# Scores as native float32 products in two 64-row halves, in place of split float32r products

## The chip, the cores and the metric

The kernel runs on one core of a Trainium2 chip. The metric is the device time of one execution in microseconds (us); the time given is the median of the timed runs. PE is TensorE (its products), PEld its weight loads, DVE is VectorE, ACT ScalarE, POOL GpSimd, SP the sync engine, from whose queue the kernel issues its DMAs.

## The reference

Attention with a threshold over 4 batches of 8 heads (576 tokens, 64 columns), then a gated product with four weights, then a mixture of eight experts over all 2304 tokens.

```
scores = q @ k.T / sqrt(64)                          # per head, 576 x 576
thresh = max(scores, axis=-1) - tau
scores = where(scores >= thresh, scores, -1e9)
attn   = exp(scores - max(scores))
out    = attn / (sum(attn) + 1e-9) @ v               # 576 x 64 per head
x = out of all heads side by side                    # 2304 x 512
x = ((x @ w1) * (x @ w2)) @ w3 @ w_out
out = sum over 8 experts e: P[:, e] * (relu(x @ W1[e]) @ W2[e])
      # P from x @ w_gate, normalised over rows and columns 8 times
```

Everything is float32 at the inputs and the output (w1, w2, w3 and w_out are float64 and are turned into float32 on the chip).

## The kernel before

Two heads are one pair; there are 16 pairs. The 576 query rows of each head are cut into four tiles of 128 rows, and what is left of both heads (64 rows each) makes a ninth tile of 128 rows. So a pair is nine tiles, t = 0 to 8, and the attention part runs 144 steps, one per tile, after which the mixture stages follow. All instructions stand in an order written out by hand: each engine works through its own list in order, and a letter string, `ORDER`, says in which order the parts of a step are issued. The parts of one step belong to different tiles: in step s the mask of tile s (`mask`), the scores, the row maximum, the threshold and the exponential of tile s + 2 (`scores`, `rowmax`, `thresh`, `expo`), the transposes of tile s - 1 (`transp`, evacuated by `evac`), the transposes of the last 64 columns of three tiles (`tails`, every third step), the product with the values (`pv`, in steps t = 0, 2, 3, 5 and 7) and the spreading of the sums (`spread`, t = 2 and 8). The sum over the values (`vsum`) stands behind step t = 1.

On TensorE a step thus runs: transposes t (L205), scores s (L160), now and then rb (L281), tt (L216) and pv (L251), the filler products w (L487), and vs (L228). On VectorE it runs: the mask (L180), the reciprocal (L199), a piece of a weight's conversion to float32 (lines 516 to 524, one in most steps by `CONVERT`), the row maximum (L165), some of the parts of `prep`, and the product x (L300). The scores of two tiles have a PSUM buffer each, of two banks: the left 288 keys in one bank, the right 288 in the other. The scores of tile s + 2 wait until the mask of tile s has read its buffer.

A score in float32 accuracy is made of float32r products, which take fewer passes than float32 ones. Each head's q and k arrive with their 64 columns twice, on partitions 0 to 63 and 64 to 127. ScalarE rounds k to float32r (kh, L137) and GpSimd subtracts (kl, L140; VectorE does the very first). ScalarE writes q/8 rounded to float32r on all 128 partitions of qs (L129), and VectorE turns the lower 64 into the remainder (L133, two halves of 288 columns a head). One product of qs with kh and one with kl over 128 rows then give a block of 288 keys: four products a tile, and eight for the ninth tile, whose two heads accumulate into one result; for that, qs has 64 columns of zeros between the heads, and head 1's q is rotated by 64 rows in the input's layout. The parts of `prep` for pair n + 1 are spread over the steps of pair n by `PREP`: GpSimd's in t = 3 and 6, VectorE's (L133) in t = 4, 5, 7 and 8, ScalarE's in t = 0, 1, 4 and 5. `load` (L96, DMAs at L106) fetches q for pair n + 2 at t = 2 and k at t = 4, two DMAs each of 288 KB. Before the first step pair 0 is loaded in eight smaller DMAs, one head's k and q after the other, and pair 1 behind them.

Beside the attention, `W34` converts the float64 weights and multiplies w3 by w_out in small portions, spread over the steps.

Of the kernel before, what the change touches and what calls it, by code (L numbers as in the profile page):

```python
# [9 lines left out]
F32 = mybir.dt.float32  # L10
F32R = mybir.dt.float32r
AF = mybir.ActivationFunctionType
ALU = mybir.AluOpType
# [6 lines left out]
B, H, S, D = 4, 8, 576, 64  # L20
DM, DFF, E = 512, 1024, 8
NTOK = B * S
NP = B * H // 2
# [1 line left out]
SB = 768  # L25
HT = SB // 2
NSB = NTOK // SB
QW = 2 * S + 64

SPLITS_AT = ((0, 0), (1, 1), (2, 2), (3, 3), (8, 4), (9, 5), (10, 6))  # L30

# [1 line left out]

CONVERT = (1, 0, 1, 1, 1, 2, 1, 1, 1, 1, 1, 1, 1, 1, 2, 2, 1, 1)
PRODUCTS = (0, 4, 0, 0, 4, 0, 1, 0, 5, 0, 3, 0, 1, 4, 0, 2, 1, 4)
ORDER = "TfmzeiSVsqIovgrcxRltXyw"
PREP = {0: (4,), 1: (0,), 3: (6,), 4: (2, 1), 5: (3, 5), 6: (7,), 7: (8,), 8: (9,)}
PD = 2
SHARE = 2.0
AHEAD = {-2: 1, -1: 2, 0: 1, 1: 1, 2: 3, 3: 1, 4: 1, 5: 1, 6: 1, 7: 1}  # L40
# [11 lines left out]
def tile_of(n, t):  # L52

    return TILES[min(n, 1)][t]
# [9 lines left out]
def f32(ap):  # L64
    return ap.bitcast(F32)
# [6 lines left out]
def attention(k):  # L72

    tc, nc = k.tc, k.nc
# [3 lines left out]
    epool = early.enter_context(tc.tile_pool(name="atte", bufs=1))  # L78
# [14 lines left out]

    raws, sets = {}, {}

    def load(n, i):  # L96
        if n >= NP:
            return
        t = epool.tile([128, 2, S], F32, tag=f"r{i}", name=f"r{i}_{n}", bufs=2)
        raws[n, i] = t  # L100
        if n:
            fetch(n, i, slice(0, 2))

    def fetch(n, i, h):
        for half in range(2):
            nc.sync.dma_start(raws[n, i][64 * half:64 * half + 64, h], k.qk[n, :, 2 * i + h.start:2 * i + h.stop])  # L106

    def load_v(n):
        if n >= NP:
# [2 lines left out]
        nc.sync.dma_start(rv, k.vv[n])  # L112
        raws["v", n] = rv

    def prep(n, part):
        if n >= NP:
            return
        rq, rk = raws[n, 0], raws[n, 1]
        if n not in sets:
            qs = epool.tile([128, QW], F32R, tag="qs", name=f"qs{n}", bufs=2)  # L120
            kh = epool.tile([128, 2, S], F32R, tag="kh", name=f"kh{n}", bufs=2)
            kl = epool.tile([128, 2, S], F32R, tag="kl", name=f"kl{n}", bufs=2)
            sets[n] = (qs, kh, kl)
            nc.gpsimd.memset(f32(qs[:, S:S + 64]), 0.0)
        qs, kh, kl = sets[n]
        qcol = (slice(0, S), slice(S + 64, QW))
        if part in (0, 1):
            h = part
            nc.scalar.activation(qs[:, qcol[h]], rq[:, h], AF.Copy, scale=0.125)  # L129
        elif part in (2, 3, 8, 9):  # L130
            h, o = part % 2, 0 if part < 4 else 288
            dst = qs[64:128, qcol[h].start + o:qcol[h].start + o + 288]
            nc.vector.scalar_tensor_tensor(  # L133
                out=dst, in0=rq[64:128, h, o:o + 288], scalar=0.125, in1=f32(dst), op0=ALU.mult, op1=ALU.subtract)
        elif part in (4, 5):
            h = part - 4
            nc.scalar.activation(kh[:, h], rk[:, h], AF.Copy)  # L137
        elif part in (6, 7):
            h = part - 6
            (nc.gpsimd if n or h else nc.vector).tensor_tensor(out=kl[:, h], in0=rk[:, h], in1=f32(kh[:, h]), op=ALU.subtract)  # L140

    spool, ppool, tpool, outs = {}, {}, {}, {}

    def scores(s):
        if s >= NT:
            return
        n, t = divmod(s, 9)
        qs, kh, kl = sets[n]
        ps = psums.tile([128, 2, 512], F32, tag="s", name=f"s{s}", bufs=2)
        spool[s] = ps  # L150
        h, i = tile_of(n, t)
        if h is None:
            todo = [(512, 0), (576, 1)]
        else:
            todo = [((QW - 512 if h else 0) + 128 * i, h)]
        for c in range(2):
            cols = slice(288 * c, 288 * c + 288)
            ops = [(q0, h, kk) for q0, h in todo for kk in (kh, kl)]
            for i, (q0, h, kk) in enumerate(ops):
                nc.tensor.matmul(ps[:, c, 0:288], lhsT=qs[:, q0:q0 + 128], rhs=kk[:, h, cols],  # L160
                                 start=i == 0, stop=i == len(ops) - 1)

    def rowmax(s):
        ps = spool[s]
# [129 lines left out]
    def x_out(s):  # L294
        if (nj := due(s, "y")) is None:
# [4 lines left out]
        nc.vector.tensor_tensor(out=k.x[:, c0, S * b + q:S * b + q + m], in0=outs.pop((n, j))[:, 0:m],  # L300
                                in1=outs.pop(("r", n, j))[:, 0:m], op=ALU.mult)

    load(0, 1)
    load(0, 0)
    for h in range(2):
        fetch(0, 1, slice(h, h + 1))
        fetch(0, 0, slice(h, h + 1))
    nc.sync.dma_start(k.ntau, k.tau.to_broadcast([128, 1]))
    nc.scalar.activation(thr[:, 0:1], k.ident[:, 0:1], AF.Exp)
    fill = W34(k, epool, wpool, psum)  # L310
    load(1, 0)
    load(1, 1)
    for part in (4, 6, 0, 2):
        prep(0, part)
    nc.scalar.mul(k.ntau, k.ntau, -1.0)
    load_v(0)
    scores(0)
# [1 line left out]
    for s in range(2):  # L319
        rowmax(s)  # L320
        thresh(s)
        expo(s)
    for part in (1, 3, 5, 7):
        prep(0, part)

    def parts(s, which):
        n, t = divmod(s, 9)
        for part in PREP.get(t, ())[which]:
            prep(n + 1, part)

    def tiles(f, d):

# [2 lines left out]
    def groups(f, d):  # L335
# [6 lines left out]
        "q": groups(tails, 3), "l": groups(tail_out, 3), "v": pv,  # L342
        "V": spread, "I": repeat, "o": spread_out, "y": x_out, "f": lambda s: fill.out(),
        "c": lambda s: fill.convert(s, 2 if s < RAMP else CONVERT[s % 18]), "z": lambda s: fill.convert(s, 0),
        "r": lambda s: parts(s, slice(0, 1)), "R": lambda s: parts(s, slice(1, 9)), "w": lambda s: fill.mms(s)}
    ahead = iter(())
    for s in range(NT + 10):
        n, t = divmod(s, 9)
        if s == NT - 20:
            k.raw0 = wpool.tile([128, 4, 256], F32, name="raw1_0")  # L350
            nc.sync.dma_start(k.raw0.rearrange("p a b -> p (a b)"), k.wab["a"][0])
        if s >= NT - 2 and k.moe is None and fill.gen is None:
            early.close()
            k.moe = Moe(k)
            ahead = k.moe.run()
        if s == NT:
            banks.close()
            k.moe.banks()
        if s == NT + 1:
            assert fill.done()  # L360
            parts34.close()
            k.moe.grow()
        for what in ORDER:
            if what in steps:
                steps[what](s)
        if s < 2:
            prep(0, (9, 8)[s])
        if n < NP and t in (2, 4):
            load(n + 2, t // 2 - 1)
        if (s - SUMS_AT) % 9 == 0 and 0 <= s - SUMS_AT < NT:  # L370
            vsum((s - SUMS_AT) // 9)
        if n < NP and t == VALUES_AT:
            load_v(n + 1)
        if k.moe:
            for _ in range(AHEAD.get(s - NT, 0)):
                next(ahead)
# [7 lines left out]
class W34:  # L384
# [28 lines left out]
    def load(self, j):  # L413
        if j >= len(self.chunks):
            return
        raw = self.pool.tile([128, 512, 2], I32, tag="wraw", name=f"wraw{j}", bufs=2)
        self.k.nc.sync.dma_start(raw.rearrange("p a b -> p (a b)"), self.source(j).bitcast(I32))
        self.raw[j] = raw
# [544 lines left out]
def _layouts(np, inputs):  # L963

    c = np.ascontiguousarray
    pairs = lambda a: a.reshape(NP, 2, S, D)
    q = pairs(inputs["q"])
    q = np.stack([q[:, 0], np.roll(q[:, 1], 64, axis=1)], axis=1)
    qk = c(np.concatenate([a.transpose(0, 3, 1, 2) for a in (q, pairs(inputs["k"]))], axis=2))
    v = pairs(inputs["v"])  # L970
    vv = c(np.concatenate([v[:, :, :512].reshape(NP, 2, 4, 128, D), np.concatenate([v[:, :, 512:], np.zeros_like(v[:, :, 512:])], axis=2)[:, :, None]],
                          axis=2).transpose(0, 3, 1, 2, 4))
# [32 lines left out]
```

## Time and profile before

| | us |
|---|---|
| median of 3 runs (2286.64 to 2288.07) | 2287.48 |
| the profiled execution | 2283.88 |
| its span, first to last instruction | 2281.8 |
| mask of the first tile starts | 12.27 |
| mask of the last tile starts | 448.18 |

| engine | busy us | share of the span |
|---|---|---|
| PE | 2171.4 | 95% |
| PEld | 1945.2 | 85% |
| DVE | 1272.9 | 56% |
| ACT | 971.9 | 43% |
| POOL | 1074.0 | 47% |

The page of a profile gives one execution. Busy time of PE runs from the start of a product to its modelled end, and products overlap, so a busy PE isn't PE at its peak. L160 is line 160 of the kernel. In the views by line, "idle before" is the time in which the engine stood still ahead of these instructions, and the arrow names what ended it. Timelines merge equal neighbours (x16) and give the start of the first and the time until the end of the last.

### The profile page before, as it was taken

To read this page: it belongs to the slowest core of one execution; us is meant where nothing else is said; L and a number is where in the kernel's file an instruction comes from. 1 tells how busy PE (TensorE), PEld (TensorE's weight loads), DVE (VectorE), ACT (ScalarE), POOL (GpSimd) and SP (SyncE) were. 2 spreads that over 40 slices of the span, in tenths; PEclk is the share of its full clock that TensorE was granted. 3 is DMA by queue.
4 is the path that set the end of the run, shared out by engine and by line. 5 is a ranking of instruction groups with operands and counts; after the bars stand their busy time and mean duration, and the time that the engine had idled before them with its cause. 6 is when DMAs were issued, how large, how long until landed. Compare 5 with 4: busy or idle time off the path is not lost.

```text
span 2281.8 us, 32262 instructions
## 1 busy us (share of the span) xinstructions
PE 2171.4 (95%) x12624; PEld 1945.2 (85%) x12624; DVE 1272.9 (56%) x2175; ACT 971.9 (43%) x1805; POOL 1074.0 (47%) x1029
## 2 busy tenths in 40 slices
PE   6788888899999999999999999999999999999999
PEld 5677777788989888999999899999999899999998
DVE  7898988756464565444444644444445544444444
ACT  6787788743222333333333433333334333333332
POOL 4665666575010444444445544444446544444442
PEclk9999999999999999999999999999999999999999
DMA  5344344165435121211211211211211211211211
GB/s 145 100 118 133 111 137 128 48 254 189 189 148 189 49 73 56 75 66 65 74 65 65 102 66 64 74 66 64 74 68 63 102 67 64 74 69 61 74 69 43
DMA packets 57432, 213.39 MB, mean 94 GB/s; under 512 B 7104, under 2 KB 7104, under 8 KB 57280
## 3 DMA queue, kind: packets, MB, share of 16 engines
q1 hardware_dynamic: 57280, 211.33, 27.3%
q8 instruction: 99, 1.62, 0.3%
q14 instruction: 53, 0.43, 0.1%
HBM read 185.61 MB, written 25.69 MB: 93 GB/s over the span
## 4 chain that ended last, share of the span: by engine, by line
PE 69%; DVE 1%; issue 0%; ACT 0%; POOL 0%; DVEq 0%; ACTq 0%
PE ye L749 36%; PE py L679 19%; PE px L679 14%; DVE xl L668 0%; PE py L828 0%; DVE c L723 0%; PE px L828 0%; DVE c L734 0%; DVE prob L866 0%; ACT xh L667 0%; DVE acc L803 0%; POOL w1l L623 0%; DVE hl L745 0%; POOL w1l L620 0%; DVE small L863 0%
## 5 line engine op out<-in xcount | busy, mean ns | idle before, releaser
L749 PE MATMUL ye<-w2h,hl 128*128 128x512 f32 x1152 | 451.2, 392 | 0.0
L749 PE MATMUL ye<-w2h,hh 128*128 128x512 f32 x1152 | 451.1, 392 | 0.0
L749 PE MATMUL ye<-w2l,hh 128*128 128x512 f32 x1152 | 450.8, 391 | 0.0
L744 ACT ACTIVATE hh<-c 128x384 fp32r<-128x384 f32 x288 | 151.5, 526 | 611.0 <-DVE c L723 611.0
L625 POOL TENSOR_TENSOR w1l<-wt,w1h 128x1024 fp32r<-128x1024 f32 x104 | 252.6, 2429 | 285.4 <-ACT w1h L622 284.9
L679 PE MATMUL py<-xh,w1h 128*128 128x384 f32 x960 | 322.8, 336 | 7.5 <-DVE c L723 3.6
L679 PE MATMUL py<-xl,w1h 128*128 128x384 f32 x960 | 322.8, 336 | 3.5 <-DVE xl L668 3.5
L679 PE MATMUL py<-xh,w1l 128*128 128x384 f32 x960 | 322.0, 335 | 0.0
L620 POOL TENSOR_TENSOR w1l<-raw,w1h 128x256 fp32r<-128x256 f32 x104 | 79.2, 762 | 479.3 <-ACT w1h L614 479.3
L679 PE MATMUL px<-xh,w1h 128*128 128x384 f32 x720 | 242.6, 337 | 5.5 <-ACT p L703 2.8
L679 PE MATMUL px<-xl,w1h 128*128 128x384 f32 x720 | 242.1, 336 | 2.7 <-DVE xl L668 2.7
L749 PEld LDWEIGHTS ye<-w2l,hh 128*128 128x128 f32 x1152 | 216.3, 188 | 32.6
L749 PEld LDWEIGHTS ye<-w2h,hl 128*128 128x128 f32 x1152 | 216.2, 188 | 32.6
L679 PE MATMUL px<-xh,w1l 128*128 128x384 f32 x720 | 241.7, 336 | 0.0
L749 PEld LDWEIGHTS ye<-w2h,hh 128*128 128x128 f32 x1152 | 216.3, 188 | 24.6 <-ACT x L775 0.2
L679 PEld LDWEIGHTS py<-xh,w1h 128*128 128x128 f32 x960 | 180.2, 188 | 31.2 <-DVE c L723 6.5
L679 PEld LDWEIGHTS py<-xl,w1h 128*128 128x128 f32 x960 | 180.1, 188 | 22.3 <-DVE xl L668 5.3
L706 DVE TENSOR_TENSOR u<-py,p 128x384 f32<-128x384 f32 x120 | 66.8, 556 | 216.9 <-PE py L679 214.8
L160 PE MATMUL s<-kh,qs 128*128 128x288 f32 x320 | 106.5, 349 | 77.6 <-DVE p L180 70.5
L679 PEld LDWEIGHTS py<-xh,w1l 128*128 128x128 f32 x960 | 180.1, 188 | 0.0
L613 POOL TENSOR_TENSOR wt<-raw 128x512 f32<-128x512 f32 x104 | 139.4, 1340 | 76.9 <-DMA raw<-in_e 61.1
L745 DVE SCALAR_TENSOR_TENSOR hl<-c,hh 128x384 fp32r<-128x384 f32 x288 | 166.1, 577 | 9.3
(142 smaller groups left out, 4166.9 us busy)
## 6 DMA issues: line engine op xcount, KB each, us to landing
raw<-in_e SPq DMA_DIRECT2D x192, 512.0 KB, 4.0
r<-in_qk SPq DMA_DIRECT2D x60, 288.0 KB, 5.8
wraw<-in_w SPq DMA_DIRECT2D x32, 512.0 KB, 3.6
w1h<-w_kept SPq DMA_DIRECT2D x16, 896.0 KB, 5.0
w1l<-w_kept SPq DMA_DIRECT2D x16, 896.0 KB, 6.9
w_kept<-w1h SPq DMA_DIRECT2D x8, 896.0 KB, 7.9
w_kept<-w1l SPq DMA_DIRECT2D x8, 896.0 KB, 9.0
raw<-w SPq DMA_DIRECT2D x12, 512.0 KB, 3.6
```

The lines of the kernel that those rows point to most:

```text
L160: nc.tensor.matmul(ps[:, c, 0:288], lhsT=qs[:, q0:q0 + 128], rhs=kk[:, h, cols], start=i == 0, stop=i == len(ops) - 1)
L613: nc.gpsimd.tensor_tensor(out=t[:, 0:2], in0=raw[:, 1:3], in1=raw[:, 0:2], op=ALU.subtract)
L620: nc.gpsimd.tensor_tensor(out=wl[:, 0], in0=raw[:, 0], in1=f32(wh[:, 0]), op=ALU.subtract)
L625: nc.gpsimd.tensor_tensor(out=wl[:, 3:7], in0=t, in1=f32(wh[:, 3:7]), op=ALU.subtract)
L679: self.nc.tensor.matmul(out, lhsT=w[:, wi, o], rhs=x[xi][:, d], start=n == 0 and not adds, stop=n == 5, skip_group_check=True)
L706: tt(out=self.u2, in0=py, in1=self.p1, op=ALU.add)
L744: nc.scalar.activation(hi, src, AF.Relu)
L745: self.later.append(lambda: nc.vector.scalar_tensor_tensor(out=lo, in0=src, scalar=0.0, in1=f32(hi), op0=ALU.max, op1=ALU.subtract))
L749: self.queue.append((out.shape[-1], lambda: self.nc.tensor.matmul(out, lhsT=l, rhs=r, start=start, stop=stop, skip_group_check=True)))
```

## The change

q is used as it is loaded, k is scaled by 1/8 on its way through ScalarE, and both stay float32. The 64 rows of a head's k lie on partitions 0 to 63 for the first 288 keys and on 64 to 127 for the last 288, so k takes half the memory; q still lies on both. A tile's scores are two float32 products, one over partitions 0 to 63 into the first bank, one over 64 to 127 into the second; the ninth tile's are four, of 64 query rows each. The kernel's pv and vs are native float32 products already. `prep` is one ScalarE copy a pair, at t = 5; L133, L140 and the zero columns are gone. `load` fetches q and k of pair n + 1 at t = 1, in four DMAs; before the first step nothing of pair 1 is loaded; and step "R" of `ORDER` is gone.

```diff
@@ -25,7 +25,7 @@
 SB = 768
 HT = SB // 2
 NSB = NTOK // SB
-QW = 2 * S + 64
+KH = S // 2
 
 SPLITS_AT = ((0, 0), (1, 1), (2, 2), (3, 3), (8, 4), (9, 5), (10, 6))
 
@@ -33,8 +33,8 @@
 
 CONVERT = (1, 0, 1, 1, 1, 2, 1, 1, 1, 1, 1, 1, 1, 1, 2, 2, 1, 1)
 PRODUCTS = (0, 4, 0, 0, 4, 0, 1, 0, 5, 0, 3, 0, 1, 4, 0, 2, 1, 4)
-ORDER = "TfmzeiSVsqIovgrcxRltXyw"
-PREP = {0: (4,), 1: (0,), 3: (6,), 4: (2, 1), 5: (3, 5), 6: (7,), 7: (8,), 8: (9,)}
+ORDER = "TfmzeiSVsqIovgrcxltXyw"
+LOAD_AT, KEYS_AT = 1, 5
 PD = 2
 SHARE = 2.0
 AHEAD = {-2: 1, -1: 2, 0: 1, 1: 1, 2: 3, 3: 1, 4: 1, 5: 1, 6: 1, 7: 1}
@@ -93,17 +93,20 @@
 
     raws, sets = {}, {}
 
-    def load(n, i):
+    def load(n):
         if n >= NP:
             return
-        t = epool.tile([128, 2, S], F32, tag=f"r{i}", name=f"r{i}_{n}", bufs=2)
-        raws[n, i] = t
+        raws["q", n] = epool.tile([128, 2, S], F32, tag="rq", name=f"rq{n}", bufs=2)
+        raws["k", n] = epool.tile([128, 2, KH], F32, tag="rk", name=f"rk{n}", bufs=1)
         if n:
-            fetch(n, i, slice(0, 2))
-
-    def fetch(n, i, h):
+            fetch(n, slice(0, 2))
+
+    def fetch(n, h):
         for half in range(2):
-            nc.sync.dma_start(raws[n, i][64 * half:64 * half + 64, h], k.qk[n, :, 2 * i + h.start:2 * i + h.stop])
+            rows = slice(64 * half, 64 * half + 64)
+            nc.sync.dma_start(raws["k", n][rows, h], k.qk[n, :, 2 + h.start:2 + h.stop, KH * half:KH * half + KH])
+        for half in range(2):
+            nc.sync.dma_start(raws["q", n][64 * half:64 * half + 64, h], k.qk[n, :, h])
 
     def load_v(n):
         if n >= NP:
@@ -112,32 +115,12 @@
         nc.sync.dma_start(rv, k.vv[n])
         raws["v", n] = rv
 
-    def prep(n, part):
+    def prep(n, h):
         if n >= NP:
             return
-        rq, rk = raws[n, 0], raws[n, 1]
         if n not in sets:
-            qs = epool.tile([128, QW], F32R, tag="qs", name=f"qs{n}", bufs=2)
-            kh = epool.tile([128, 2, S], F32R, tag="kh", name=f"kh{n}", bufs=2)
-            kl = epool.tile([128, 2, S], F32R, tag="kl", name=f"kl{n}", bufs=2)
-            sets[n] = (qs, kh, kl)
-            nc.gpsimd.memset(f32(qs[:, S:S + 64]), 0.0)
-        qs, kh, kl = sets[n]
-        qcol = (slice(0, S), slice(S + 64, QW))
-        if part in (0, 1):
-            h = part
-            nc.scalar.activation(qs[:, qcol[h]], rq[:, h], AF.Copy, scale=0.125)
-        elif part in (2, 3, 8, 9):
-            h, o = part % 2, 0 if part < 4 else 288
-            dst = qs[64:128, qcol[h].start + o:qcol[h].start + o + 288]
-            nc.vector.scalar_tensor_tensor(
-                out=dst, in0=rq[64:128, h, o:o + 288], scalar=0.125, in1=f32(dst), op0=ALU.mult, op1=ALU.subtract)
-        elif part in (4, 5):
-            h = part - 4
-            nc.scalar.activation(kh[:, h], rk[:, h], AF.Copy)
-        elif part in (6, 7):
-            h = part - 6
-            (nc.gpsimd if n or h else nc.vector).tensor_tensor(out=kl[:, h], in0=rk[:, h], in1=f32(kh[:, h]), op=ALU.subtract)
+            sets[n] = epool.tile([128, 2, KH], F32, tag="ks", name=f"ks{n}", bufs=2)
+        nc.scalar.activation(sets[n][:, h], raws["k", n][:, h], AF.Copy, scale=0.125)
 
     spool, ppool, tpool, outs = {}, {}, {}, {}
 
@@ -145,20 +128,16 @@
         if s >= NT:
             return
         n, t = divmod(s, 9)
-        qs, kh, kl = sets[n]
+        q, kk = raws["q", n], sets[n]
         ps = psums.tile([128, 2, 512], F32, tag="s", name=f"s{s}", bufs=2)
         spool[s] = ps
         h, i = tile_of(n, t)
-        if h is None:
-            todo = [(512, 0), (576, 1)]
-        else:
-            todo = [((QW - 512 if h else 0) + 128 * i, h)]
         for c in range(2):
-            cols = slice(288 * c, 288 * c + 288)
-            ops = [(q0, h, kk) for q0, h in todo for kk in (kh, kl)]
-            for i, (q0, h, kk) in enumerate(ops):
-                nc.tensor.matmul(ps[:, c, 0:288], lhsT=qs[:, q0:q0 + 128], rhs=kk[:, h, cols],
-                                 start=i == 0, stop=i == len(ops) - 1)
+            rows = slice(64 * c, 64 * c + 64)
+            for g in range(2) if h is None else (h,):
+                out = ps[64 * g:64 * g + 64] if h is None else ps
+                cols = slice(512, S) if h is None else slice(128 * i, 128 * i + 128)
+                nc.tensor.matmul(out[:, c, 0:KH], lhsT=q[rows, g, cols], rhs=kk[rows, g], start=True, stop=True)
 
     def rowmax(s):
         ps = spool[s]
@@ -300,18 +279,13 @@
         nc.vector.tensor_tensor(out=k.x[:, c0, S * b + q:S * b + q + m], in0=outs.pop((n, j))[:, 0:m],
                                 in1=outs.pop(("r", n, j))[:, 0:m], op=ALU.mult)
 
-    load(0, 1)
-    load(0, 0)
+    load(0)
     for h in range(2):
-        fetch(0, 1, slice(h, h + 1))
-        fetch(0, 0, slice(h, h + 1))
+        fetch(0, slice(h, h + 1))
     nc.sync.dma_start(k.ntau, k.tau.to_broadcast([128, 1]))
     nc.scalar.activation(thr[:, 0:1], k.ident[:, 0:1], AF.Exp)
     fill = W34(k, epool, wpool, psum)
-    load(1, 0)
-    load(1, 1)
-    for part in (4, 6, 0, 2):
-        prep(0, part)
+    prep(0, slice(0, 1))
     nc.scalar.mul(k.ntau, k.ntau, -1.0)
     load_v(0)
     scores(0)
@@ -320,13 +294,12 @@
         rowmax(s)
         thresh(s)
         expo(s)
-    for part in (1, 3, 5, 7):
-        prep(0, part)
-
-    def parts(s, which):
+    prep(0, slice(1, 2))
+
+    def keys(s):
         n, t = divmod(s, 9)
-        for part in PREP.get(t, ())[which]:
-            prep(n + 1, part)
+        if t == KEYS_AT:
+            prep(n + 1, slice(0, 2))
 
     def tiles(f, d):
 
@@ -342,7 +315,7 @@
         "q": groups(tails, 3), "l": groups(tail_out, 3), "v": pv,
         "V": spread, "I": repeat, "o": spread_out, "y": x_out, "f": lambda s: fill.out(),
         "c": lambda s: fill.convert(s, 2 if s < RAMP else CONVERT[s % 18]), "z": lambda s: fill.convert(s, 0),
-        "r": lambda s: parts(s, slice(0, 1)), "R": lambda s: parts(s, slice(1, 9)), "w": lambda s: fill.mms(s)}
+        "r": keys, "w": lambda s: fill.mms(s)}
     ahead = iter(())
     for s in range(NT + 10):
         n, t = divmod(s, 9)
@@ -363,10 +336,8 @@
         for what in ORDER:
             if what in steps:
                 steps[what](s)
-        if s < 2:
-            prep(0, (9, 8)[s])
-        if n < NP and t in (2, 4):
-            load(n + 2, t // 2 - 1)
+        if n < NP and t == LOAD_AT:
+            load(n + 1)
         if (s - SUMS_AT) % 9 == 0 and 0 <= s - SUMS_AT < NT:
             vsum((s - SUMS_AT) // 9)
         if n < NP and t == VALUES_AT:
@@ -965,7 +936,6 @@
     c = np.ascontiguousarray
     pairs = lambda a: a.reshape(NP, 2, S, D)
     q = pairs(inputs["q"])
-    q = np.stack([q[:, 0], np.roll(q[:, 1], 64, axis=1)], axis=1)
     qk = c(np.concatenate([a.transpose(0, 3, 1, 2) for a in (q, pairs(inputs["k"]))], axis=2))
     v = pairs(inputs["v"])
     vv = c(np.concatenate([v[:, :, :512].reshape(NP, 2, 4, 128, D), np.concatenate([v[:, :, 512:], np.zeros_like(v[:, :, 512:])], axis=2)[:, :, None]],
```

## Rows read from the trace of the kernel before

**Rows 1.** Busy time by stage ("windows"): length, each engine's busy time (instructions), TensorE's clock, DMA.
```profile
45.70:420.00 374.30, 315.83 (x2935) 266.02 (x2934) 331.46 (x639) 300.30 (x638) 225.82 (x323) 0.99 0.42 118
```

**Rows 2.** Groups by line, 45.7 to 420 us: count | busy us, mean ns | idle before.
```profile
L165 DVE TENSOR_REDUCE nmx<-s 128x1 f32<-128x576 f32 x125 | 94.0, 752 | 38.4 <-PE s L160 38.1
L160 PE MATMUL s<-kh,qs 128*128 128x288 f32 x278 | 90.1, 341 | 57.2 <-DVE p L180 57.1
...
L133 DVE SCALAR_TENSOR_TENSOR qs<-r,qs 64x288 fp32r<-64x288 f32 x55 | 38.9, 708 | 1.7
```

**Rows 3.** Timeline of TensorE, steps t = 0 to 5: start us, length us, what.
```profile
213.29 0.40 PE L160 MATMUL s<-kh,qs 128*128 128x288 f32 x1 [0.56 <-DVE p L180]
...
217.34 1.25 PE L228 MATMUL vs<-rv,last 128*65 128x128 f32 x10
...
219.63 0.27 PE L281 MATMUL rb<-ident,rin 128*128 128x128 f32 x1
219.83 1.09 PE L251 MATMUL pv<-pt,rv 128*64 128x128 f32 x16
...
224.43 0.30 PE L160 MATMUL s<-kl,qs 128*128 128x288 f32 x1
...
226.94 0.40 PE L160 MATMUL s<-kh,qs 128*128 128x288 f32 x1 [0.86 <-DVE p L180]
...
227.45 0.29 PE L160 MATMUL s<-kl,qs 128*128 128x288 f32 x1
```

**Rows 4.** Timeline of TensorE, cut at 219.845 and at 220.0 us.
```profile
219.83 0.33 PE L251 MATMUL pv<-pt,rv 128*64 128x128 f32 x2
...
219.83 0.44 PE L251 MATMUL pv<-pt,rv 128*64 128x128 f32 x4
```

**Rows 5.** Timeline of VectorE, steps t = 4 to 8 of the same pair.
```profile
223.91 0.46 DVE L133 SCALAR_TENSOR_TENSOR qs<-r,qs 64x288 fp32r<-64x288 f32 x1
...
225.01 0.75 DVE L165 TENSOR_REDUCE nmx<-s 128x1 f32<-128x576 f32 x1
...
227.41 0.43 DVE L524 TENSOR_SCALAR cvs<-cvq 128x512 int32<-128x512 int32 x1
227.77 0.76 DVE L165 TENSOR_REDUCE nmx<-s 128x1 f32<-128x576 f32 x1
...
233.43 1.34 DVE L133 SCALAR_TENSOR_TENSOR qs<-r,qs 64x288 fp32r<-64x288 f32 x1
...
235.22 0.74 DVE L165 TENSOR_REDUCE nmx<-s 128x1 f32<-128x576 f32 x1
...
236.73 0.90 DVE L133 SCALAR_TENSOR_TENSOR qs<-r,qs 64x288 fp32r<-64x288 f32 x1
...
238.99 0.74 DVE L165 TENSOR_REDUCE nmx<-s 128x1 f32<-128x576 f32 x1
```

**Rows 6.** Timeline of TensorE: the last score products of t = 7 and 8.
```profile
233.27 0.29 PE L160 MATMUL s<-kl,qs 128*128 128x288 f32 x1
...
237.26 0.30 PE L160 MATMUL s<-kl,qs 128*128 128x288 f32 x1
```

**Rows 7.** Timelines of GpSimd and VectorE: operations that ran beside one another.
```profile
203.64 1.41 POOL L140 TENSOR_TENSOR kl<-r,kh 128x576 fp32r<-128x576 f32 x1
203.72 1.62 DVE L524 TENSOR_SCALAR cvs<-cvq 128x512 int32<-128x512 int32 x1
...
232.69 1.76 POOL L436 TENSOR_TENSOR w3l<-wf,w3h 128x512 fp32r<-128x512 f32 x1
```

**Rows 8.** Timelines of ScalarE and VectorE at the start.
```profile
9.66 0.72 ACT L173 ACTIVATE e<-s,nmx 128x576 f32<-128x576 f32 x1
...
12.27 0.82 DVE L180 SCALAR_TENSOR_TENSOR p<-s,thr,e 128x576 f32<-128x576 f32 x1
...
18.61 0.68 ACT L137 ACTIVATE kh<-r 128x576 fp32r<-128x576 f32 x1 [6.28 <-DMA r<-in_qk]
...
21.76 0.82 DVE L180 SCALAR_TENSOR_TENSOR p<-s,thr,e 128x576 f32<-128x576 f32 x1
```

## The prediction

> **What bounds the kernel now.** I read the busy time by stage first: between 45.7 and 420 us VectorE is busy 331.5 of 374.3 us, TensorE 315.8, ScalarE 300.3 and GpSimd 225.8, with TensorE granted 0.99 of its clock [rows 1]. No engine is full, so the order inside a step decides. 125 tiles take 374.3 us: 2.99 us a step, 27 us a pair of heads (nine steps, t = 0 to 8). After 450 us the mixture stages follow; the change touches nothing there, so I let a gain or loss of the attention part shift the end one for one.
>
> The groups by line say what a step holds on VectorE: the mask and the row maximum, and between them fillers, among which L133, the low half of q: 0.71 us in the mean, 38.9 us in this stretch [rows 2]. The row maximum of tile s+2 follows the mask of tile s: the mask frees the bank, TensorE computes the scores, VectorE reads them. VectorE waited 38.1 us for scores ahead of the row maximum, TensorE 57.1 us for the mask [rows 2]. So each waits for the other, and the timelines show where.
>
> From 213.29, where TensorE waits 0.56 us for the mask of step t = 0, to 226.1 it has no gap; then it waits 0.86 us [rows 3]. Steps t = 0 to 3 are thus TensorE's: transposes, score products, the sums over values (vs, pv) and the filler products w fill them, and VectorE waits. In t = 4 to 8 the products wait for the mask, and VectorE's fillers set the pace. L133 stands only in t = 4, 5, 7 and 8.
>
> **The change, part by part.**
>
> *Score products.* Now one tile takes four passes of 288 columns, 0.13 us apart; from first start to last end 226.94 to 227.74, 0.80 us [rows 3]. A native float32 product runs as two passes: vs, five products in the code, shows ten passes in 1.25 us, the last of 0.27, so (1.25 - 0.27)/9 = 0.109 us for 128 columns [rows 3], hence 0.245 for 288. Four such passes a tile are 0.98 us one after another, 0.49 if the two row halves run together. No row shows row halves. The nearest are the column halves of pv: 16 passes in 1.09 us [rows 3]; the first two start together, the next two 0.11 us later [rows 4]. Taken singly they would need 16 x 0.109 and the last one's 0.16 us beyond it, 1.9 us. I take the same for row halves: 0.49 us against 4 x 0.133 = 0.53. The last tile of a pair (t = 8), eight passes now, should also take 0.49, as four quarters.
>
> "TensorE: Matmul & The Clock Gate" of the Trainium skill (Part 3, The mechanism) says that products stay in program order in start and end, and that only weight loads are pulled ahead. By that rule the second pass of one half would stand in front of the other half's first, and a tile would take 0.735 us; the pairs of pv start together instead, though the code writes them in the same order. I keep 0.49 and make 0.735 a rival.
>
> *Switching the array's shape.* From rb (full array) to pv the next start comes 0.20 us later instead of 0.11, and the first pass lasts 0.33 instead of 0.27 us [rows 3, 4]: 0.15 us a switch. Score products are now neighbours of full-array work (t before; tt, w or rb behind), so the change adds two switches a step, one where pv follows. Bounds: nothing, if row halves beside the full array cost none, and 0.30 a step. I take 0.29, nearly the row's. In t = 0 to 3 it lies open: 0.15 behind the first product, three times 0.29, 0.15 ahead of that of t = 4, less 4 x 0.04 for the shorter products and 0.08 for the last one's end: +0.93 us a pair, +15 us over 16 pairs. In t = 4 to 8 it lies in the wait for the mask; there the scores arrive slightly earlier (0.06 + 0.245 + 0.41 = 0.71 against 0.80), -2 us where they will be last.
>
> *L133 goes (60 in the pairs' steps, 4 at the start).* It is worth only what stands behind the scores' end. In the steps of one pair: t = 4, scores end 224.73, row maximum 225.01, slack 0.28; t = 5, 227.74 and 227.77, 0.03; t = 7, 233.56 and 235.22, 1.66; t = 8, 237.56 and 238.99, 1.43 [rows 3, 5, 6]. With L133 at its plain 0.46 [rows 5] that frees 0.28 + 0.03 + 0.46 + 0.46 = 1.23 us a pair; at its stretched 1.34 and 0.90 in t = 7 and 8 [rows 5] it is 2.55. Over 15 pairs 18 to 38 us. The stretched ones run beside a GpSimd operation: the 1.34 ends 0.3 us behind a 1.76 us subtraction that began at 232.69 [rows 5, 7]. That operation stays, and the conversion next in line works in the same memory, so I take the lower end and a little: 20 us.
>
> "SBUF — State Buffer" of the Trainium skill (§ SBUF: two separate sides) calls the port pair that VectorE and GpSimd share an exclusive lock, held for the whole instruction. By it the conversion inherits the wait, and the gain is 18 us; the rows of the stretch agree.
>
> *GpSimd and ScalarE.* The subtractions for kl leave GpSimd, two a pair. One of 1.41 us stretched the conversion at 203.72 to 1.62 us; such a conversion takes 0.43 alone [rows 5, 7]. Four such stood in t = 6 over the stage, so -4 us (0 to -7). ScalarE keeps one copy a pair instead of four; its queue is 80% busy and last nowhere but at the start, I count nothing.
>
> *Loads.* Four a pair, 864 KB for 1152 KB, issued at t = 1; the keys' copy comes four steps (12 us) later, and the sync queue passes nothing that waits for these buffers. I count nothing.
>
> *The start.* The mask of tile 0 stood at 12.27, behind an L133 that waited for ScalarE, while its exponentials ended at 10.38 [rows 8]: -1.9 us. Then ScalarE waited 6.28 us for the second pair's keys, to 18.61, with the next thresholds behind it [rows 8]. That load now comes later and its copy at t = 5; the first two steps took 9.5 us from mask to mask [rows 8] and should take about 6.5: -3 us. Together -5 (-2 to -7).
>
> *Sum.* +15 - 2 - 20 - 4 - 5 = -16 us. The profiled execution took 2283.9 us (2281.8 of it span) and would take 2267.9; the median shown is 3.6 us above it, so 2271.5.
>
> **Rivals.**
>
> *The halves overlap by one pass* (a tile takes 0.735): +0.245 in the 64 steps of t = 0 to 3 and in about 20 others, where the fillers are now short: +20, 2291.5, no change. For it: no row of row halves, and the order of the code. Against: the pairs of pv.
>
> *The halves run singly*, the case on the other side: a tile takes 0.98 us instead of 0.49. In t = 0 to 3 that is 0.49 x 64 = +31 us; in t = 4 to 8 about 31 of the 75 steps have fillers too short to hide it: +15. Sum -16 + 46 = +30, 2317. It decides from the point where the second half starts 0.17 us behind the first: 0.17 x (64 + 31) = 16. For it: no row of row halves either, and a product over 64 rows takes as many columns as one over 128. Against, again pv.
>
> *Switches cost nothing and the stretch of L133 vanishes*: -15 for the switches and up to -15 more for L133, 2242 to 2256. For it: the switch is priced by column halves. Against: GpSimd's operations stay.
>
> *The granted clock falls to 1.2 GHz* in the attention part, half the array being idle in each product: TensorE's 316 us of work there would double, some +260 us. Against: pv uses half the columns in each product, at 0.99 [rows 1].
>
> **How the numbers follow.** Forecast 0.62 (faster, its own range 2262 to 2281); cheaper switches 0.10 (faster); overlap by one pass 0.11 (no change, within 0.2%, 4.6 us, about what a measurement can tell); single halves 0.14 (slower); clock 0.03 (slower). The forecast's own spread and the upper edge of the overlap put a little on either neighbour: faster 0.70, same 0.12, slower 0.18. The range reaches from cheaper switches, 2254, to the overlap by one pass, 2291.
>
> **What would show it.** Score passes of about 0.41 us (now 0.30), four a tile, in pairs that start within 0.02 us; first start to last end about 0.71 us. Behind them the next start 0.09 us late. VectorE's wait ahead of the row maximum above 38 us, since t = 0 to 3 get longer by 0.9 us a pair, and t = 4 to 8 shorter by 1.6 us. First mask near 10.4 us; the attention part ends some 16 us earlier. I am wrong if the second half starts behind the first one's passes, or if t = 4 to 8 keep their length because conversions take over the whole wait for GpSimd.

## The result, and the profile after

The changed kernel takes 2253.26 us (median of 4 runs, 2252.92 to 2253.43) against 2287.06 of the kernel before on the same chip (4 runs, 2284.71 to 2288.07): a ratio of 0.9853, 95% interval 0.9836 to 0.9871, 33.8 us faster. The forecast was 2271.5, 16 us faster, with 2254 as the lower end of its range. The direction was right, and so was the account of the products; the gain is twice the forecast, and the time lies 0.7 us below the range. In the two profiled executions the difference is 30.7 us, since that of the kernel before (2283.88) is 3.2 us below its median.

Where it came from is read from the starts of the masks (time from the span's start, us):

| mask of tile | before | changed | difference |
|---|---|---|---|
| 0 | 12.27 | 10.45 | -1.8 |
| 9 (second pair) | 46.81 | 37.17 | -9.6 |
| 135 (last pair) | 425.02 | 392.88 | -32.1 |
| 143 (last tile) | 448.18 | 416.94 | -31.2 |
| span | 2281.8 | 2251.1 | -30.7 |

So all of it is in the attention part: 9.6 us up to the first mask of the second pair, 1.6 us in each of the 14 pairs that follow; the last pair, which prepares none, is 0.9 us longer. Busy time by stage, of the changed kernel, pairs 2 to 15 (the columns are those of [rows 1]):

```profile
37.17:392.88 355.71, 327.84 (x2967) 224.76 (x2968) 287.86 (x589) 278.17 (x602) 178.20 (x287) 1.00 0.40 117
```

TensorE is busy 92% of the stretch (84% in [rows 1]), VectorE 81% (89%). The groups by line, 40 to 390 us, answer to [rows 2]:

```profile
L144 DVE TENSOR_REDUCE nmx<-s 128x1 f32<-128x576 f32 x124 | 93.6, 755 | 66.0 <-PE s L140 66.0
L140 PE MATMUL s<-ks,rq 64*128 64x288 f32 x440 | 83.1, 455 | 25.6 <-DVE p L159 25.2
```

The waits have changed sides: VectorE now waits 66.0 us for scores (38.1 before, over 374 us), TensorE 25.2 us for the mask (57.1). The products themselves, in the timeline of TensorE (cut at 202.09 for the first row):

```profile
202.07 0.51 PE L140 MATMUL s<-ks,rq 64*128 64x288 f32 x2
...
202.07 0.76 PE L140 MATMUL s<-ks,rq 64*128 64x288 f32 x4
202.76 0.50 PE L458 MATMUL w<-wol,w3h 128*128 128x512 f32 x1
```

Two passes have started by 202.09, one per half, as in [rows 4]: the halves run together. A tile takes 0.76 us from first start to last end (0.80 before, 0.71 forecast). VectorE in steps t = 6 and 7 of the eighth pair, that of [rows 5]:

```profile
207.03 1.07 DVE L487 TENSOR_SCALAR cva<-wraw 128x512 int32<-128x512 int32 x1
208.13 0.69 DVE L490 SCALAR_TENSOR_TENSOR cva<-wraw,cva 128x512 int32<-128x512 int32 x1
...
210.15 1.23 DVE L493 SCALAR_TENSOR_TENSOR cvq<-cvq,cva 128x512 f32<-128x512 f32 x1
```

Conversions of 0.42 and 0.69 us still last 1.07 and 1.23 here and there, beside an operation of GpSimd. Added up over 47 to 395 us, what VectorE's fillers last beyond their unhindered length (0.46 us for L133, 0.42 or 0.69 for the conversions) fell from 40 us (L133 12.5, the four conversion instructions 27.5) to 21 us.

### The profile page after: what moved, and what is told of

Its sections match the earlier page's. It is cut to its first block, busy times and chain, and to the rows that moved or that the text cites. A ratio compares the mean times of both kernels' runs of the same rounds, so it can differ in the third digit from the quotient of the medians.

```text
span 2251.1 us, 32102 instructions
## 1 busy us (share of the span) xinstructions
PE 2177.1 (97%) x12624; PEld 1891.9 (84%) x12624; DVE 1217.1 (54%) x2110; ACT 943.0 (42%) x1758; POOL 1019.4 (45%) x982
## 4 chain that ended last, share of the span: by engine, by line
PE 70%; DVE 1%; issue 0%; ACT 0%; POOL 0%; DVEq 0%; ACTq 0%
PE ye L720 36%; PE py L650 19%; PE px L650 14%; DVE xl L639 0%; PE py L799 0%; DVE c L694 0%; PE px L799 0%; DVE c L705 0%; DVE prob L837 0%; ACT xh L638 0%; DVE acc L774 0%; POOL w1l L594 0%; DVE hl L716 0%; POOL w1l L591 0%; DVE small L834 0%
## 5 line engine op out<-in xcount | busy, mean ns | idle before, releaser
L720 PEld LDWEIGHTS ye<-w2l,hh 128*128 128x128 f32 x1152 | 216.3, 188 | 32.6
L720 PEld LDWEIGHTS ye<-w2h,hl 128*128 128x128 f32 x1152 | 216.2, 188 | 32.6
L720 PEld LDWEIGHTS ye<-w2h,hh 128*128 128x128 f32 x1152 | 216.3, 188 | 24.7 <-ACT x L746 0.2
L650 PEld LDWEIGHTS py<-xh,w1h 128*128 128x128 f32 x960 | 180.3, 188 | 31.3 <-DVE c L694 6.4
L715 ACT ACTIVATE hh<-px 128x384 fp32r<-128x384 f32 x96 | 47.2, 492 | 272.8 <-PE px L650 272.8
```

The lines of the kernel that those rows point to most:

```text
L650: self.nc.tensor.matmul(out, lhsT=w[:, wi, o], rhs=x[xi][:, d], start=n == 0 and not adds, stop=n == 5, skip_group_check=True)
L715: nc.scalar.activation(hi, src, AF.Relu)
L720: self.queue.append((out.shape[-1], lambda: self.nc.tensor.matmul(out, lhsT=l, rhs=r, start=start, stop=stop, skip_group_check=True)))
```

## The experiments

Times are medians; "before" on the same chip took 2286.0 to 2287.3 each time. Each kernel is the changed one or the one before with the edit shown. For several of them the mean length of a step in us (mask to mask, in the 14 pairs from tile 9 to 135, pairs 2 to 15), which leaves the start aside, says more than the total:

| step t | 0 to 3 together | 4 | 5 | 6 | 7 | 8 | pair |
|---|---|---|---|---|---|---|---|
| before | 10.80 | 3.23 | 2.51 | 3.43 | 3.53 | 3.51 | 27.0 |
| changed | 11.51 | 3.00 | 2.35 | 2.96 | 2.57 | 3.01 | 25.4 |
| before without L133 | 10.70 | 2.81 | 2.38 | 4.03 | 2.42 | 3.28 | 25.6 |
| before without kl | 11.12 | 3.23 | 2.49 | 3.44 | 3.14 | 3.51 | 26.9 |
| before without either | 10.70 | 2.81 | 2.38 | 3.01 | 2.65 | 2.87 | 24.4 |

**L133 put back into the changed kernel.**

```diff
+        if n < NP - 1 and t in (4, 5, 7, 8):
+            h, o = {4: (0, 0), 5: (1, 0), 7: (0, 288), 8: (1, 288)}[t]
+            dst = dq[64:128, h, o:o + 288]
+            nc.vector.scalar_tensor_tensor(out=dst, in0=dum[64:128, h, o:o + 288], scalar=0.125, in1=f32(dst), ...)
```

It stands at step "r" of `ORDER`, and works on scratch tiles (their lines are left out here and below).

> The changed kernel (2253.3 us) with VectorE's work for the low half of q put back: 60 subtractions of 64 x 288, in t = 4, 5, 7 and 8 ahead of the conversion, as L133 stood, on a scratch tile (nothing reads them). Theory: L133 and the stretch that it shares with GpSimd were the largest part of the gain, more than the 20 us of the prediction: +22 to +27 us, 2275 to 2280. Rival: L133 was hidden behind the wait for the scores and the gain is from products and loads: under +8, at most 2261.

2284.7 (ratio to before 0.9993, 0.9984 to 1.0003): +31.4, more than the 22 to 27 us of the theory, and far from the rival. Steps t = 4, 7 and 8 go back to 3.22, 3.40 and 3.51. So with this work back on VectorE next to nothing of the gain is left.

**kl put back.**

```diff
+        if n < NP - 1 and t in (3, 6):
+            nc.gpsimd.tensor_tensor(out=dk[:, t // 6], in0=dum[:, t // 6], in1=f32(dk[:, t // 6]), op=ALU.subtract)
```

> The changed kernel with GpSimd's work for kl put back: 30 subtractions of 128 x 576 in t = 3 and 6, on a scratch tile. Theory: the conversions on VectorE that stood behind kl are worth 4 to 8 us: 2257 to 2261. Rival: GpSimd's relief carries what the prediction missed (17 us): 2268 or more.

2276.5 (9 runs, 2271.2 to 2285.1; 0.9961, 0.9946 to 0.9977): +23.2, the rival's size. Step t = 6 goes from 2.96 to 3.93 us, t = 8 from 3.01 to 3.33. The nine runs spread with the clock that TensorE was granted: 2271.2 us at 0.994 of full speed (the profiled run, +17.9), 2285.1 at 0.989, where the changed kernel always had 0.998. More on that below.

**All the splitting work put back** (both edits above and three ScalarE copies a pair).

> The changed kernel with all the splitting work put back on scratch tiles: the two above and 45 ScalarE copies of 128 x 576 (t = 0, 1 and 4). What is left of the change is the products, their switches and the loads. Theory: the work costs about 30 us, 2283: products with switches cost some 10 us, the start gives back as much, and all the gain is in the work. Rival: the float32 products themselves are the gain (no split operands to wait for): at most 2268.

2304.9 (1.0077, 1.0060 to 1.0094), 18.7 us slower than before. Both expectations missed: with equal work on the other engines the products, with their switches, cost 19 us net of what the start gives back (3.4 us at the mask of tile 9). By the steps' medians, t = 0 to 3 take 11.45 us against 10.55 before, +0.90 a pair. Here too the clock has a share: 0.991 in the median of the runs, 0.994 before.

**Before without L133, without kl, and without either.**

The first `return` alone, the second with the last edit, and all three:

```diff
         elif part in (2, 3, 8, 9):
+            return
...
         elif part in (6, 7):
+            return
...
-            ops = [(q0, h, kk) for q0, h in todo for kk in (kh, kl)]
+            ops = [(q0, h, kk) for q0, h in todo for kk in (kh, kh)]
```

> The kernel before without L133 (the lower 64 partitions of qs keep the rounded q). Theory: as the steps t = 4 to 8 are VectorE's, this alone gives -20 to -27 us, 2260 to 2267, and by the prediction's working -18 to -22. Rival: without kl's removal the conversions take over the wait for GpSimd and it gives -12 or less: 2275 or more.

> The kernel before without the subtractions for kl alone (L133 stays). Theory: with L133 in place they are worth little, -4 to -8 us (2278 to 2282), against 17 to 23 in the changed kernel: the two hide one another. Rival: kl costs the same 17 us in both: 2270 or less.

> The kernel before without L133 and without the subtractions for kl (the second product of each pair reads kh again; ScalarE's four copies, the four passes a tile and the loads stay as before). Theory: the two together are worth -40 to -46, since without L133 the subtractions stretch the conversions behind them; so 2241 to 2247, less than the changed kernel, whose products then cost about 10 us net of its better start. Rival: the float32 products in halves give part of the gain; then this stays above the changed kernel, 2255 or more.

| | us | ratio to before | difference |
|---|---|---|---|
| without L133 | 2262.0 | 0.9901 (0.9876 to 0.9926) | -24 |
| without kl | 2279.6 | 0.9967 (0.9956 to 0.9978) | -7 |
| without either | 2243.6 | 0.9809 (0.9792 to 0.9827) | -43 |

The first expectation of each held in its number. The parts add up to 31, together they give 43. Two things stand behind these numbers. The first is the stretch: in the table of steps t = 6 takes 3.43 before, 4.03 without L133, 3.44 without kl, 3.01 without either. In the kernel without L133, the conversion meets a subtraction that started 0.02 us ahead of it (timelines of GpSimd and VectorE):

```profile
216.24 1.42 POOL L141 TENSOR_TENSOR kl<-r,kh 128x576 fp32r<-128x576 f32 x1
...
216.26 1.95 DVE L520 SCALAR_TENSOR_TENSOR cva<-wraw,cva 128x512 int32<-128x512 int32 x1
```

The same conversion of the same step without either:

```profile
205.34 0.69 DVE L521 SCALAR_TENSOR_TENSOR cva<-wraw,cva 128x512 int32<-128x512 int32 x1
```

Stretch of VectorE's conversions, as above: 27.5 us before, 37 without L133 (they inherit 10 of L133's 12.5), 25 without either.

The second is TensorE's clock. In the kernel without L133, TensorE waits 1.83 us for the mask behind that long step t = 6; from 221.0 to 224.5 us it is granted 1.2 GHz, and t = 8 takes 4.46 us, with TensorE busy all through. In the kernel without either, the same step takes 3.00 us at full speed (timeline of TensorE; stages of both):

```profile
219.67 0.40 PE L161 MATMUL s<-kh,qs 128*128 128x288 f32 x1 [1.83 <-DVE p L181]
...
221.26:225.72 4.46, 4.46 (x26) 3.73 (x23) 3.07 (x6) 2.31 (x5) 3.21 (x6) 0.64 0.01 2
...
209.63:212.63 3.00, 2.89 (x19) 2.37 (x19) 3.00 (x7) 2.48 (x6) 2.76 (x4) 1.00 0.01 3
```

The kernels differ in how often this happens. For an estimate at full clock, each step of pairs 2 to 15 that ran in part at 1.2 GHz is replaced by the median of the same step in the other odd, or even, pairs (the conversions repeat every two pairs):

| pairs 2 to 15 of the trace | us | of these at 1.2 GHz | estimate at full clock | against before |
|---|---|---|---|---|
| before | 378.2 | 6.8 | 375.7 | |
| without L133 | 358.7 | 13.7 | 353.0 | -22.7 |
| without kl | 377.0 | 23.9 | 367.4 | -8.3 |
| without either | 341.9 | 0 | 341.9 | -33.8 |
| changed | 355.7 | 0 | 355.7 | -20.0 |
| changed, L133 put back | 382.6 | 6.8 | 380.4 | +4.7 |
| changed, kl put back | 372.2 | 10.2 | 367.5 | -8.2 |

At full clock the two parts add up to 31.0 us and give 33.8 together, so they hide little of one another. Most of the 12 us between 31 and 43 goes with the clock: either removal alone leaves stretches at 1.2 GHz, both together leave none. No run held the clock fixed, so this stays an estimate.

The kernel without either is also 9.7 us faster than the changed one: what the float32 products cost, net of what the later and smaller loads and three ScalarE copies fewer a pair give back. No run tried those copies by themselves.

**kl put elsewhere.** The edit of kl put back, with `t in (1, 2)`.

> The changed kernel with the same 30 GpSimd subtractions as in the run with kl back (which cost 23 us in t = 3 and 6), but in t = 1 and 2, where VectorE waits for TensorE's scores after its conversion. Theory: they cost by stretching VectorE's conversions where VectorE sets the pace; here the stretch falls into a wait: 0 to +6 us, 2253 to 2259. Rival: GpSimd's own queue is the cost (its sums, flags and repeats come late): +15 or more, 2268.

2257.3 (0.9868, 0.9852 to 0.9885): +4.0 instead of +23.2. The pair takes 25.54 us (25.41 without them); in the trace the first two pairs, with 13.7 us at 1.2 GHz, are 4.9 us longer, and the 13 after them together 0.5. Its one run at a granted clock of 0.998 took 2255.0, +1.7. The conversions are stretched as much (31.3 us over the stage, 31.6 with kl in t = 3 and 6). In the rows the conversion meets the GpSimd operation that the subtraction has pushed back, but a wait for the scores stands behind it (timelines, t = 2):

```profile
199.39 1.42 POOL L308 TENSOR_TENSOR dk<-dum,dk 128x576 fp32r<-128x576 f32 x1
200.77 1.27 POOL L502 TENSOR_TENSOR cvl<-cvl,cvs 128x512 f32<-128x512 f32 x1
...
200.82 1.50 DVE L493 TENSOR_SCALAR cva<-wraw 128x512 int32<-128x512 int32 x1
...
202.53 0.76 DVE L148 TENSOR_REDUCE nmx<-s 128x1 f32<-128x576 f32 x1 [0.20 <-PE s L144]
```

So it is the stretch that costs, where VectorE sets the pace, and not GpSimd's queue.

**One half for both products, and all rows.**

```diff
-            rows = slice(64 * c, 64 * c + 64)
+            rows = slice(0, 64)           # the other kernel: slice(0, 128)
```

> The changed kernel with both products of a tile on the same 64 rows (partitions 0 to 63, so both read the first half of the keys): the halves can't overlap, everything else is the same. Theory: the overlap is real and needed: a tile takes 0.49 us more of TensorE, 64 steps of t = 0 to 3 and some of the others pay it: +40 to +50 us, 2293 to 2303, slower than the kernel before. Rival: the attention part has room on TensorE, the overlap is worth under 15 us: at most 2268.

> The changed kernel with both products of a tile over all 128 rows (each sums over both halves of the keys' memory, so the scores are others): four passes in a row as in the run above, but no change of the array's shape around them except at the ninth tile. Theory: the switches cost 0.29 us in the four steps t = 0 to 3 and part of t = 4, so this is 14 to 20 us faster than the run above. Rival: switches are free beside row halves: within 4 us of the run above.

2348.5 (1.0257, 1.0220 to 1.0295) and 2287.0 (1.0003, 0.9993 to 1.0012). Both theories had the direction and missed the size: +95 us instead of 40 to 50, and 61.5 us between the two instead of 14 to 20. The timelines of TensorE around one tile, one half first, then all rows:

```profile
259.70 0.60 PE L184 MATMUL t<-ident,p 128*128 128x128 f32 x4
260.23 1.23 PE L140 MATMUL s<-ks,rq 64*128 64x288 f32 x4
261.39 0.44 PE L260 MATMUL rb<-ident,rw 128*128 128x128 f32 x2
```

```profile
210.54 0.60 PE L184 MATMUL t<-ident,p 128*128 128x128 f32 x4
210.97 1.14 PE L140 MATMUL s<-ks,rq 128*128 128x288 f32 x4
211.94 0.38 PE L260 MATMUL rb<-ident,rw 128*128 128x128 f32 x2
```

From t to the product 0.53 us with switch, 0.43 without; from the product to rb 1.16 and 0.97: together 0.29 us for two switches up to the start of rb, the forecast's value. From one half to two (rows above): 1.16 against 0.69 us (202.07 to 202.76), so the overlap gives back 0.47. Undisturbed pairs take 29.3, 27.5 and 25.2 us (one half, all rows, changed): 1.8 a pair for the switches, 4.1 for the overlap, 61 us over 15 pairs where the prediction's rival had 46. Most of the rest of the 95 us of one half lies in its first five pairs (39.3, 40.5, 37.5, 32.6 and 33.5 us), with TensorE's clock low:

```profile
20.00:190.00 170.00, 160.90 (x912) 108.38 (x912) 93.74 (x195) 94.93 (x202) 65.65 (x102) 0.72 0.26 76
```

**The start.** Three kernels moved the second pair's loads or copies. In the kernel before, k's first copy from t = 0 to t = 2, in all pairs (first expectation) and in the first pair alone (second); in the changed kernel, the second pair's loads ahead of the first step and its copy at t = 0 (third):

```diff
-PREP = {0: (4,), 1: (0,), 3: (6,), 4: (2, 1), 5: (3, 5), 6: (7,), 7: (8,), 8: (9,)}
+PREP = {1: (0,), 2: (4,), 3: (6,), 4: (2, 1), 5: (3, 5), 6: (7,), 7: (8,), 8: (9,)}
...
     fill = W34(k, epool, wpool, psum)
+    load(1)
...
-        if t == KEYS_AT:
+        if t == (KEYS_AT if n else 0):
```

> The kernel before (2287.1 us) with one ScalarE copy moved: k of the next pair's first head is rounded at t = 2 and not at t = 0, so that in the first pair ScalarE does not stand waiting for that load. Theory: that wait of 6.28 us is most of what the start gave (9.6 us by the mask of tile 9): -4 to -7 us, 2280 to 2283. Rival: the start's gain is from TensorE's clock, which went up at 19.6 us and stayed up after, against 29.1 us with a fall at 32.5 before: 0 to -2, 2285 to 2287.

> The kernel before with the first copy of the second pair's k moved from t = 0 to t = 2 in the first pair only (all other pairs as before). Theory: the mask of tile 9 comes 3 us earlier and the end as much, 2282 to 2284. Rival: the time is given back before tile 9 (the same steps then wait for TensorE at its lower clock): 2286 or more.

> The changed kernel with the second pair's q and k loaded before the first step and its k copied at t = 0, as the kernel before did. Theory: the later load is worth the 4.9 us by which the first pair of the changed kernel is shorter than that of the kernel without splits, since ScalarE (or TensorE, for the values) then waits for DMA again: mask of tile 9 near 42 us, 2258. Rival: the first pair is shorter for the clock and the fewer products' operands: 2253 to 2254.

2297.0 (1.0044, 1.0029 to 1.0059, slower; neither expectation held): the first pair is 3.2 us shorter, but t = 4 of all pairs grows from 3.23 to 3.70, so the run says nothing on the start. In the first pair alone: 2286.2 (0.9999, 0.9989 to 1.0009), nothing, as the rival said; mask of tile 9 at 47.31. Its timeline of TensorE shows one wait that took the place of ScalarE's:

```profile
20.43 2.40 PE L228 MATMUL vs<-rv,last 128*65 128x128 f32 x10 [1.64 <-DMA rv<-in_vv]
```

The values of the first pair were issued behind the second pair's q and k, so they land late too. The rival's reason, TensorE at its lower clock, isn't ruled out: 10.2 us of this pair ran at 1.2 GHz after the first rise, 6.8 before. The third: 2255.2 (0.9862, 0.9847 to 0.9876), +2.0, between its two expectations, mask of tile 9 at 39.32 (37.17). It waits for both again, ScalarE for k and TensorE for the values:

```profile
14.02 0.68 ACT L123 ACTIVATE ks<-rk 128x576 f32<-128x576 f32 x1 [2.45 <-DMA rk<-in_qk]
...
17.23 2.37 PE L207 MATMUL vs<-rv,last 128*65 128x128 f32 x10 [1.24 <-DMA rv<-in_vv]
```

but 2.45 us for k instead of 6.28 [rows 8] (7.39 in the kernel without splits, whose mask of tile 9 starts at 42.02). I read the difference as k being half as large and first in the queue now; no run tried that by itself.

**Less on TensorE in t = 1 to 3.** pv straight behind the scores (first), vs from t = 1 to t = 4 and the filler products of t = 4 later (second), the filler products of t = 1 later (third):

```diff
-ORDER = "TfmzeiSVsqIovgrcxltXyw"
+ORDER = "TfmzeiSvVsqIogrcxltXyw"
...
-SUMS_AT, VALUES_AT = 1, 4
+SUMS_AT, VALUES_AT = 4, 4
-PRODUCTS = (0, 4, 0, 0, 4, 0, 1, 0, 5, 0, 3, 0, 1, 4, 0, 2, 1, 4)
+PRODUCTS = (0, 4, 0, 0, 0, 0, 4, 1, 5, 0, 4, 0, 0, 0, 0, 4, 2, 5)     # second
+PRODUCTS = (0, 1, 0, 0, 4, 0, 4, 1, 5, 0, 1, 0, 0, 4, 0, 4, 2, 5)     # third
```

> The changed kernel with pv issued straight behind the scores, ahead of tt and rb: in t = 0, 2 and 3 one change of the array's shape of three goes (scores, pv, full array, for scores, full array, pv, full array). Theory: steps t = 0 to 3 are TensorE's, so 3 x 0.15 x 16 = -7 us, 2246. Rival: TensorE's wait just moves (VectorE or the transposes are last there): 0 to -2, 2251 to 2253.

> The changed kernel with work of TensorE moved out of t = 1 to 4: the sum over the values (vs, 1.1 us) from t = 1 to t = 4 and the filler products of t = 4 (0.9 us) to t = 6 and 7. Theory: t = 1 is TensorE's and t = 6 has room, so t = 1 falls from 2.99 to about 2.4 us and nothing else grows: -0.6 a pair, -9 us, 2244. Rival: steps 2 and 3 are set by ScalarE's evacuations, which stay: 0 to -3 us, 2250 to 2253.

> The changed kernel with only the filler products moved, from t = 1 (4 and 3 of them, now 1) to t = 6 and 7, vs left at t = 1. Theory: as TensorE is last in t = 1 to 3 and has room in t = 6, 0.6 us a pair goes, as in the run with vs moved (-4.7): 2247 to 2249. Rival: in t = 6 and 7 they push the transposes and pv back and half is lost: 2251 or more.

2260.9 (0.9890, 0.9872 to 0.9909): 7.6 slower than the changed kernel. A switch goes, but rb ends later, and ScalarE, whose queue holds the evacuation of rb ahead of conversion and threshold, stands (its timeline, t = 2 and 3); t = 3 grows from 2.96 to 3.44 us.

```profile
203.68 0.38 ACT L268 ACTIVATE xo<-rb 128x256 f32<-128x256 f32 x1 [1.81 <-PE rb L260]
```

The second: 2248.6 (0.9832, 0.9817 to 0.9847), 4.7 faster than the changed kernel and the fastest whole version here; the third: 2249.0 (0.9834, 0.9819 to 0.9849). In both only the step of vs and w gets shorter (mask to mask at t = 2 from 3.10 to 2.41 and 2.65 us), and t = 8 gets 0.2 longer. The second gave half of the 9 us expected: one of the three steps had the work that was moved, the other two hold pv. The third ends at the upper edge of its first expectation.

## Why the prediction fell short

*Score products and switches: right.* The halves start together, the four passes of a tile in two pairs 0.35 us apart, and two switches cost 0.29 us. The terms +15 and -2 (+13) stand against +14.8: the 14 pairs are 0.99 us longer than without splits (25.41 against 24.42, both all at full clock), 13.9, and the last pair 0.9. This is net of three ScalarE copies fewer a pair, which the prediction put at nothing and no run tried. The -2 for t = 4 to 8 had the wrong sign: 0.17 us a pair longer. The rival that the halves run singly was too cheap: 61 us, not 46, and the clock on top. The rival of one pass in between doesn't hold either. The prediction drew it from "TensorE: Matmul & The Clock Gate" in the Trainium skill (Part 3, The mechanism: products keep program order in start and end). The trace agrees with that order for the two products (first passes at 202.074 and 202.080, second passes at 202.420 and 202.427 us); the prediction was wrong to apply it to the passes inside them.

*GpSimd's subtractions: the step that failed.* -4 (0 to -7) was read off four stretched conversions in t = 6 of the trace of before. At full clock the estimates give 8.3 us with L133 in place, 11.1 without it (353.0 to 341.9), 11.8 put back into the changed kernel. The prediction said that the conversion next in line inherits the wait for GpSimd; it did not ask which GpSimd operation would then stand beside it. Without L133 that was kl itself in t = 6, 4.1 to 4.4 us in 11 of the 14 pairs, where the kernel without either needs 2.9 to 3.2. With the clock that falls behind these long steps, the subtractions cost 18 us (2262.0 to 2243.6), and 23 put back. That the run without kl gave -7, inside the forecast's range, is luck: the clock fell more often there (23.9 us at 1.2 GHz against 6.8) and hid a part. The exclusive lock of "SBUF — State Buffer" in the Trainium skill (§ SBUF: two separate sides) fits the rows: the conversion waits out the subtraction (216.24 + 1.42 = 217.66; 216.26 + 1.95 = 218.21). It speaks for the lower end only where the GpSimd operation stays, and kl, in two steps of nine, went.

*L133: near.* -20 was forecast; at full clock it is 22.7 us alone and 24.7 put back, and 1.9 us at the first mask, which the prediction had under the start. That conversions take over most of its stretch was right (10 of 12.5 us).

*The clock: put at nothing.* The prediction weighed only a fall. The runs of the kernel before had 0.994 in the median, those of the changed kernel 0.998: an estimate of 2.5 us in pairs 2 to 15 of the traces, and more in slower runs (2282.5 to 2286.2 us at 0.996, 2287.3 to 2292.9 at 0.990 and 0.991).

*The start: right in size.* -5 (-2 to -7) forecast, the first mask with it. That mask comes 1.8 us earlier; of the 9.6 us at the mask of tile 9 the kernel without splits has 4.8 (first mask, L133 and kl in that pair), so loads and products gave another 4.8. The reason was half right: ScalarE's wait for k was one of two waits of the same load, and moving the copy alone gave nothing.

*Sum.* +14.8 (products, switches), -4.8 (start), -42.7 (L133, kl and the clock) = -32.7, against -33.8 measured; the forecast had +13, -5, -24. That it closes is no test of its own, since the kernel without either stands between the two. In pairs 2 to 15 at full clock it is +13.8 for the products, -22.7 for L133 and -11.1 for kl. The signs expected were there in direction: TensorE's steps t = 0 to 3 longer by 0.7 us (0.93 forecast), t = 4 to 8 shorter by 2.3 us a pair where 1.6 was forecast. The rival *Switches cost nothing and the stretch of L133 vanishes* (2242 to 2256) holds the measured time, but not by its reasons: the switches were paid, and the stretch moved to the conversions until kl went too.

## What to carry to other kernels

When differences between kernels are added up, look first at the clock that each was granted: here two removals gave 24 and 7 us alone and 43 together, and at full clock 23, 8 and 34. When a change removes two pieces of work, ask of the second what it stands beside once the first is gone. Work on GpSimd is priced by the VectorE instructions that run beside it: the same 30 subtractions cost 23 us (12 at full clock) where VectorE set the pace, and 4 where it waited for TensorE anyway. When a wait for a load is moved away, look at the transfer issued behind it: here it was late next.

## What the runs showed of the hardware

Native float32 products over the two 64-row halves run side by side: four passes of 288 columns take 0.69 us from the first start to the next product, 1.16 on one half. A change of the array's shape around them cost 0.145 us each way.

TensorE's clock: with both products on one half TensorE was busy 160.9 of 170 us between 20 and 190 us and was granted 0.72 of full speed (part of the time at 1.2 GHz, the rest at 2.4); with all rows it was granted 1.00 over 180 to 450 us, busy 256.8 of 270. The changed kernel stayed at 1.00 from 37 to 417 us; the kernel before, which waited 57.1 us for the mask, had 0.99 [rows 1]. A fall inside the pairs was paid: 4.46 us for a step of 3.00. In the first pair a later rise to 2.4 GHz made no difference that can be seen: 26.72 us in the changed kernel and 26.80 with vs moved, whose records of full speed begin 9.1 and 15.8 us into the pair.
